# A gated mix of a state-space layer and linear attention: the skip term of seven late tiles moves from TensorE to VectorE, three more tiles are transposed by TensorE, and the late order is written anew

## The chip, the cores and the metric

The kernel runs on one core of one Trainium2 chip. The metric is the device time of one execution in microseconds (us), the median of several runs. The profile is of one execution, recorded by the hardware. A core has four engines that compute, each with its own queue worked off in order: TensorE (PE in the profile; PEld is its weight load), VectorE (DVE), ScalarE (ACT) and GpSimd (POOL). SyncE (SP) issues DMAs here; ScalarE and GpSimd issue some too.

## The reference

The input x has 2048 rows of 512. Two branches are computed from it and mixed by a gate for each row. In branch a, a diagonal complex recurrence of 512 states runs over the rows and is read out by C, and x times the vector Dskip is added. In branch b, 32 heads of linear attention use softmax features of both signs.

```python
g = _sigmoid((x * gate_w).sum(-1, keepdims=True))
# branch a
Lam_bar = jnp.exp(dt * Lam)
h = Lam_bar[None, :] * h + Bu[:, t, :]          # for each row t
y = 2.0 * jnp.einsum("blp,dp->bld", hseq, Cmat).real + x * Dskip[None, None, :]
# branch b
phi_q = jnp.concatenate([_softmax(pq, axis=-1), _softmax(-pq, axis=-1)], axis=-1)
kv = jnp.einsum("bhsf,bhsd->bhfd", phi_k, v)
o = num / den
return (lambda x, *d: x.transpose(*d))(o, 0, 2, 1, 3).reshape(B, S, D) @ wo
# the mix
return g * a + (1 - g) * b
```

## The kernel before

The rows are cut into 16 tiles of 128. A tile holds every eighth row: the rows of one residue r of 8, in one half a of the sequence. So the recurrence runs over one residue only and the others follow from it by matmuls. Output tile n is tile `order[n]` of the rows; the text below numbers tiles by n.

The program is written as generators (st_y, st_o and so on), each of which yields between steps. The long string ORDER (line 24) lists the steps, and the loop at line 817 walks it: a token such as "o7" runs the next step of that generator, "@7" names the PSUM bank that the step takes, ":D" puts an eviction on VectorE (otherwise it is ScalarE's), ":A" puts an output's DMA on ScalarE's queue (otherwise SP's). The order of ORDER is the order of each engine's queue. Waits between engines are put in from what each instruction reads and writes; a bank that is taken again is waited for until its last reader is done.

The first half of ORDER makes the weights, the keys' features, the values, the recurrence and the sums kv. The late part, from about 87 us on, makes the output:

- q n: four matmuls (128 rows by 512) into PSUM, evicted to row block n of Xq (bf16, 16 blocks of 512).
- X g, N g, E g, S g: the features of a group g of four tiles, from Xq's blocks 4g to 4g+3. X and N are trees of maxima and minima and a subtraction (VectorE, lines 512, 522 and 528), E is four exponentials (ScalarE, line 139), S is a tree of sums, its logarithm "lg", a difference "dl", its exponential "rho", a product (line 560) and four DMA transposes into phT, issued by SP (line 564). Group A is tiles 0 to 3.
- y n: branch a of tile n into one PSUM bank: eight matmuls over the states in two blocks of four (line 718), then four matmuls of 128 columns with the diagonal matrices Dd, which add x times Dskip (line 723).
- o n: the attention of tile n. For each half of the heads, four narrow matmuls into pn (line 737), then "ld" (a logarithm, always ScalarE) and "nu" (a copy out of PSUM, ScalarE or, with ":D", VectorE). Then "rd" (ScalarE), "on" (VectorE, line 745), and the transpose of on: a DMA transpose issued by SP (line 759), or for the tiles in OT_PE four TensorE transposes into a bank "po" (line 754) and a copy out of it.
- t n: four matmuls with Wo add the attention into y's bank (line 766); the sum times the gate G is evicted (line 778 on ScalarE, line 780 on VectorE) and stored (line 786). Tile LAST = 14 is evicted and stored in halves, one by ScalarE (line 772) and one by VectorE (line 773).
- G: the gate's value, four small steps; Y: the masked sums kv. h, c and z finish the recurrence.

The output leaves from PSUM bank to bank: y holds its bank from its first matmul to t's eviction. Eight banks serve q, h, y, pn and po.

Of the kernel before, what the change touches and what calls it, by code (L numbers as in the profile page):

```python
# [10 lines left out]
ALU = mybir.AluOpType  # L11
# [9 lines left out]
P = 128  # L21
# [18 lines left out]
h31@6 z3 z3 sA a4 h01 h31 c6 c6 sA q13@3 q13 z3 a4 a4 Y Y h22@0 G q10 z3 z3 G q6@2 q6 h22 z3 z3 sA sA Y Y c1 c1 q9@4  # L40
q8@6 q5@7 h62@3 h41@5 c3 h41 c1 c3 c3 h13@0 h62 q11@2 h13 q11 q8 q12@1 c6 q12 h21@5 q5 h21 h02@2 c7 q4@6 q4 h53@3 h53
h23@1 h23 h33@0 h33 sA q9 h40@7 h40 sA q7@5 h43@6 h63@3 c7 h43 q7 c7 y4@0 y4 sA h63 sA h03@1 END h02 o0@4 o0 X1 N1
o1@7 o1 q14@6 X1 N1 h03 o0@5 X1 o1@2 o1 o1 o0 o0 q15@3 o2@4 o2 o2@7 o2 N1 q15 X1 N1 X1 N1 E1 E1 y2@1 y1@2 y1 E1 E1 q14
# [26 lines left out]
def kernel(  # L70
# [641 lines left out]
    def st_y(n):  # L712
        ti = order[n]
        r, a = ti // 2, ti % 2
        py = bank([P, D], F32, "py")
        live["py", n] = py
        for t in range(NT2):
            MM(out=py[:], lhsT=hs(r, t, slice(a * P, (a + 1) * P)), rhs=C2B[t], start=(t == 0), stop=False)  # L718
            if t % 4 == 3:
                yield  # L720
        for kt in range(KT):
            xs = xT[:, kt, ti * P:(ti + 1) * P]
            MM(out=py[:, kt * P:(kt + 1) * P], lhsT=xs, rhs=Dd[:, kt, :], start=False, stop=False)  # L723
# [38 lines left out]
    def st_t(n):  # L762
        ti = order[n]
        py, oT = live["py", n], live["oT", n]
        for g in range(HG):
            MM(out=py[:], lhsT=oT[:, g, :], rhs=Wo[:, g, :], start=False, stop=(g == HG - 1))  # L766
        yield
        ot = pools["op"][1].tile([P, D], BF16, name="ot", bufs=14)
        ot2 = pools["op"][1].tile([P, D], BF16, name="ot", bufs=14) if n == LAST else ot

        def ot_halves():
            nc.scalar.mul(out=ot[:, 0:D // 2], in_=py[:, 0:D // 2], mul=G[:, ti:ti + 1])
            VS(out=ot2[:, D // 2:D], in0=py[:, D // 2:D], scalar1=G[:, ti:ti + 1], scalar2=None, op0=ALU.mult)

        if n == LAST:
            ot_halves()
        elif sel["eng"] == "act":
            nc.scalar.mul(out=ot[:], in_=py[:], mul=G[:, ti:ti + 1])  # L778
        else:
            VS(out=ot[:], in0=py[:], scalar1=G[:, ti:ti + 1], scalar2=None, op0=ALU.mult)  # L780
# [80 lines left out]
```

## Time and profile before

| what | us |
|---|---|
| median of 3 runs (155.09 to 156.0) | 155.27 |
| the profiled execution | 155.2 |
| its span | 153.1 |
| TensorE, busy in the span | 147.5 |
| VectorE | 133.1 |
| ScalarE | 129.3 |
| GpSimd | 15.8 |

Rows of the profile are read as follows. A row of the timeline gives the start, the duration, the engine, the line, the operation, what it writes and reads, and in brackets how long its engine had been idle before and what ended that. A row "x4" merges four instructions that follow one another. In a row of a group, "| 3.0, 748 |" is the total in us and the mean of one in ns, and behind it stands the idle time before such instructions. A row of the DMA issues ends with the size of one in KB and the us from issue to landing. In the chain of waits each row is a start, a length and what held the end up at that time; matmuls of one kind that follow one another stand as one row, at the pace at which they follow.

### The profile page before, as it was taken

The numbers are of one execution on the slowest core, as the hardware profiler recorded it, in microseconds if no ns is written. First come the engines' busy times: TensorE is split into PE (matmuls) and PEld (weight loads), VectorE is DVE, ScalarE is ACT, GpSimd is POOL, SyncE is SP. The second block draws the span as 40 slices with busy tenths as digits, with TensorE's granted clock in tenths as the row PEclk, the third lists the DMA queues.
The fourth block names the chain that finished last, engine by engine and source line by source line (L and its number), as shares of the span: only waits on it lengthen the run. The fifth ranks groups of instructions, "written<-read, shape, count | busy, mean of one in ns | idle before, by whom it ended". The sixth has DMA issues, their size and how long they took to land.

```text
span 153.1 us, 3382 instructions
## 1 busy us (share of the span) xinstructions
PE 147.5 (96%) x1254; PEld 95.5 (62%) x1254; DVE 133.1 (87%) x304; ACT 129.3 (84%) x279; POOL 15.8 (10%) x43
## 2 busy tenths in 40 slices
PE   7999979999999999999999999999999999999990
PEld 7844434788878986869867656555555555546550
DVE  3799999999999999999999999999999858716441
ACT  3589998999998999999998999699488998618471
POOL 8239980000000000000000000000000000000000
PEclk9999999999999999999999999999999999999999
DMA  4785996494455699720000007911159959989943
GB/s 122 158 215 77 232 160 143 99 79 104 103 107 100 133 222 178 167 97 4 0 0 4 0 0 167 76 37 33 36 98 144 178 125 187 168 139 186 255 145 104
DMA packets 50992, 17.55 MB, mean 115 GB/s; under 512 B 44192, under 2 KB 50976, under 8 KB 50976
## 3 DMA queue, kind: packets, MB, share of 16 engines
q1 hardware_dynamic: 49120, 15.82, 57.0%
q10 hardware_dynamic: 1696, 1.51, 3.1%
q8 instruction: 10, 0.16, 0.5%
q0 software_dynamic: 160, 0.01, 0.2%
q14 instruction: 6, 0.05, 0.2%
HBM read 2.64 MB, written 2.10 MB: 31 GB/s over the span
## 4 chain that ended last, share of the span: by engine, by line
PE 80%; SPq 9%; DMA 8%; issue 1%; DVE 0%; ACT 0%
PE pgq L602 18%; PE py L718 16%; PE py L766 9%; PE pq L476 9%; SPq L230 7%; DMA xT<-in_A_x_dram 5%; PE pk L476 5%; PE pv L476 5%; PE ph L669 4%; DMA phT<-EEq 3%; PE kvacc L579 3%; PE pn L737 3%; PE pgq L607 2%; PE py L723 2%; PE pgq L609 2%; SPq L285 1%
## 5 line engine op out<-in xcount | busy, mean ns | idle before, releaser
L602 PE MATMUL pgq<-xT,BT 128*128 128x256 bf16 x256 | 31.5, 273 | 0.0
L476 PEld LDWEIGHTS <-xT 128*128 128x128 bf16 x192 | 18.1, 97 | 19.2 <-DMA xT<-in_A_x_dram 1.7
L602 PEld LDWEIGHTS <-BT 128*128 128x128 bf16 x256 | 24.6, 98 | 4.1
L139 ACT ACTIVATE EEk<-EEk 128x1024 bf16<-128x1024 bf16 x20 | 20.5, 1082 | 0.0
L120 ACT CAST uv<-pgq 128x512 bf16<-128x512 f32 x28 | 15.9, 605 | 0.7 <-PE pgq L602 0.5
L766 PE MATMUL py<-Wo,oT 128*128 128x512 bf16 x64 | 15.9, 380 | 0.0
L476 PE MATMUL pv<-Wv,xT 128*128 128x512 bf16 x64 | 15.8, 379 | 0.0
L476 PE MATMUL pq<-Wq,xT 128*128 128x512 bf16 x64 | 15.6, 379 | 0.0
L476 PE MATMUL pk<-Wk,xT 128*128 128x512 bf16 x64 | 14.8, 380 | 0.8 <-DMA xT<-in_A_x_dram 0.8
L139 ACT ACTIVATE EEq<-EEq 128x1024 bf16<-128x1024 bf16 x12 | 11.7, 1043 | 0.2 <-DVE EEq L528 0.2
L139 ACT ACTIVATE ld<-pn 128x16 f32<-128x16 f32 x32 | 6.1, 191 | 6.1 <-PE pn L737 4.7
L778 ACT ACTIVATE ot<-py,G 128x512 bf16<-128x512 f32 x11 | 7.4, 689 | 4.0 <-PE py L766 3.6
L591 ACT ACTIVATE phT<-X,dgB 128x512 bf16<-128x512 bf16 x16 | 10.7, 725 | 0.0
L120 ACT CAST nu<-pn 128x256 bf16<-128x256 f32 x27 | 9.9, 381 | 0.0
L745 DVE TENSOR_TENSOR on<-nu,rd 128x512 bf16<-128x512 bf16 x16 | 6.7, 421 | 3.5 <-ACT rd L139 1.8
L120 ACT CAST Xq<-pk 128x512 bf16<-128x512 f32 x15 | 8.6, 597 | 1.3 <-PE pk L476 1.3
L120 ACT CAST vx<-pv 128x512 bf16<-128x512 f32 x16 | 9.1, 603 | 0.4 <-PE pv L476 0.4
L549 DVE TENSOR_TENSOR EEk<-EEk,rck 128x4096 bf16<-128x4096 bf16 (+1 forms) x5 | 9.3, 1859 | 0.0
L120 ACT CAST Xq<-pq 128x512 bf16<-128x512 f32 x16 | 8.9, 609 | 0.2 <-PE pq L476 0.2
L766 PEld LDWEIGHTS <-oT 128*128 128x128 bf16 x64 | 5.5, 97 | 5.7 <-DMA oT<-on 0.8
L737 PEld LDWEIGHTS <-phT 128*128 128x128 bf16 x128 | 6.3, 97 | 3.5 <-DMA phT<-EEq 0.8
L512 DVE TENSOR_TENSOR smk<-smk 128x512 bf16<-128x512 bf16 (+4 forms) x18 | 8.1, 447 | 0.1
(180 smaller groups left out, 323.9 us busy)
## 6 DMA issues: line engine op xcount, KB each, us to landing
X<-HM SPq DMA_DIRECT2D x8, 256.0 KB, 4.4
out_dram<-ot SPq DMA_DIRECT2D x8, 128.0 KB, 2.2
out_dram<-ot ACTq DMA_DIRECT2D x7, 128.0 KB, 2.7
C2r<-in_B_wqkv_dram ACTq DMA_DIRECT2D x2, 256.0 KB, 3.5
Wv<-in_B_wqkv_dram SPq DMA_DIRECT2D x1, 512.0 KB, 4.1
Bn<-in_A_B_re_dram SPq DMA_DIRECT2D x1, 512.0 KB, 6.4
Bn<-in_A_B_im_dram SPq DMA_DIRECT2D x1, 512.0 KB, 7.2
Wo<-in_B_wo_dram SPq DMA_DIRECT2D x1, 512.0 KB, 4.1
```

The source lines that it names most:

```text
L120: nc.scalar.copy(out=out_ap, in_=in_ap)
L139: ins = nc.scalar.activation(**kw)
L230: nc.sync.dma_start_transpose(out=xT[:, :, ti * P:(ti + 1) * P], in_=x_res[ti // 2, ti % 2])
L476: MM(out=pt[:], lhsT=xT[:, kt, ti * P:(ti + 1) * P], rhs=W[:, kt, :], start=(kt == 0), stop=(kt == KT - 1))
L512: VT(out=dst, in0=cur[:, :, :, 0:n, :], in1=cur[:, :, :, n:2 * n, :], op=op)
L549: VT(out=E5, in0=E5, in1=rc.to_broadcast([P, L, 2 * NB, Dh, 4]), op=ALU.mult)
L591: nc.scalar.mul(out=t_, in_=x_, mul=c_)
L602: MM(out=pg[:, h, :], lhsT=BT[:, kt, 2 * j + h, :], rhs=xT[:, kt, r * NC:(r + 1) * NC], start=(h == 0 and kt == 0), stop=(r % 2 == 0 and k ...
L718: MM(out=py[:], lhsT=hs(r, t, slice(a * P, (a + 1) * P)), rhs=C2B[t], start=(t == 0), stop=False)
L737: MM(out=pn[:, 4 * m:4 * m + 4, :].rearrange("p h e -> p (h e)"), lhsT=ph[:, 4 * hf + m, :], rhs=KVm[:, 4 * hf + m, :], start=(m == 0), st ...
L766: MM(out=py[:], lhsT=oT[:, g, :], rhs=Wo[:, g, :], start=False, stop=(g == HG - 1))
L778: nc.scalar.mul(out=ot[:], in_=py[:], mul=G[:, ti:ti + 1])
```

## The change

Seven of the late tiles, SKIP_DVE = (8, 9, 10, 11, 12, 13, 15), leave out the four Dskip matmuls of y. Their term x times Dskip times G is made by VectorE: step Z n computes it from x, G and Dskip into a float32 tile that lies in blocks 8 to 15 of Xq once these are read, and the eviction of t n becomes one VectorE instruction, py times G plus that tile. The x rows and Dskip, spread over the partitions, are loaded by three DMAs on GpSimd's queue (step XL, twice in the list) into blocks 0 to 7 of Xq.

The tuple OT_PE grows by tiles 8, 9 and 10, which are transposed by TensorE rather than by DMA. ORDER is the same up to its 499th token and new from there on. Among the new places: the first XL stands ahead of END and the second ahead of group 1's last steps; Z9 stands inside S3, the other Z between tiles 8's and 15's last steps; the list ends with t14, t13 and t15, where it ended with t15 and t14.

The late list is cut to its last part, before and after:

```diff
...
-y6@7 X3 t2:A o4@2 o4 o4@5 o4 o4 y6 y6 t3 X3 o4 X3 o4 S2 S2 t3 o5@1 o5 o5@2 o5 o5 y13@5 y13 o5 N3 o6@4 S2 o6 o6@1 o6 o6
-y12@2 o5 y7@4 y7 y12 o6 o6 t4 y7 S2 S2 t4:D S2 E3 E3 E3 E3 S2 o7@1 o7 t5 t5 S3 o7@0 o7 S3 o7 t6 S3 o7 S2 o7 y8@1 o8@3
...
-o11 y15 o13@4 o13:D o13@6 t6:A o13 o13 o11 o12 y10@1 o14@4 y15 o14:D o12@6 t9 o12:D t7:A t1 y10 y10 o13 o15@4 o15
-o15@6 t4:A t5 o15 o15 t8 o15 t12 t12 t12:A t10 o14@4 o14 o14 t10:D o13@6 t11 o15@2 o15 t10 o13:D t11 t11:A y13 t13 o14
-o14@1 t15 t13 t13 t15 t15 o14:D t14 t14 t14:A
...
+h23 c7 sA q8@1 h43@0 h62@5 q12@4 h41 h43 h62 sA q7 c7 sA h03@6 q8 h21@1 h63 h03 XL h21 END y5@5 o1@2 X1 o0@6 o0 N1 o1
+y6@0 o0@6 o2@1 X1 y6 o1@2 o2 N1 X1 N1 X1 o0 q14@7 N1 o2@6 o0 o1 X1 o1 y1@2 y0@1 y1 N1 q12 XL X2 h02 q14 y4@7 o1 y2@3
...
+o4@3 o4 X3 S2 y5 y7 N3 S2 y3 o3 o5@3 o4 o4 S2 o5 N3 S1 o5@1 o5 S2 y7 S1 y14@3 t3 o6@1 S2 o5 S2 o5 E3 o6 y6 y14 o6@1 S2
+o4 t3:D y14 o5 o7@4 t4 E3 o6 y13@1 o6 t5 E3 E3 o7:D S2 t4:D y11@7 o8@4 t5 S2 o6 o8 o7@5 y11 o7 S3 o8@4 o9@5 o9 o8 o7
+Z9 S3 y13 S3 S3 o9@5 o9:D S3 o8 S3 o6 o7 S2 S3 t6 S2 S3 t6 y10@5 o10@4 o8 o10 y10 o10@4 o10:D o7 y9@0 o10 Z8 S3 o9 Z11
+o8@4 o8 y9 o11@4 o9 t8 o11 o9@4 o10 t7 t8:D S3 o9 o10@4 t9 S3 o10:D o12@4 Z12 t7 Z10 o12 o11@2 y15@6 S3 o12@4 o11:D
+o11 t10 o13@2 o11 y15 t9:D o11 t2:A t10:D t6:A o12 o14@4 o13:D o12 o14:D t0:A o14@0 o14 t9 o12 y12@5 o14 o13@4 o15@2
+o12@0 o15 o14 o12:D t1 y12 t10 t7:A t3 o13 Z13 t5 o15@2 o15:D o13 t11 o14@4 o15 o14 o13 t12 t8 o15 o15@4 t11:D t12:D
+o13@2 o15:D t4:A t14 o13 t11:A Z15 t12:A t14 t13 t15 t14:A t13:D t15:D t13 t15
-OT_PE = (12, 13, 14, 15)
+OT_PE = (8, 9, 10, 12, 13, 14, 15)
 LAST = 14
+SKIP_DVE = (8, 9, 10, 11, 12, 13, 15)
+GX_SLOT = (0, 1, 2, 3, 0, 1, 0)
...
             MM(out=py[:], lhsT=hs(r, t, slice(a * P, (a + 1) * P)), rhs=C2B[t], start=(t == 0), stop=False)
             if t % 4 == 3:
                 yield
+        if n in SKIP_DVE:
+            return
         for kt in range(KT):
             xs = xT[:, kt, ti * P:(ti + 1) * P]
             MM(out=py[:, kt * P:(kt + 1) * P], lhsT=xs, rhs=Dd[:, kt, :], start=False, stop=False)
+        yield
+
+    def st_XL():
+        rows = x2.rearrange("(a c r) d -> c a r d", r=NR, c=P)
+        nc.gpsimd.dma_start(out=Xq[:, 0:3, :], in_=rows[:, 0, 0:5:2])
+        nc.gpsimd.dma_start(out=Xq[:, 3, :], in_=A_Dskip.unsqueeze(0).to_broadcast([P, D]))
+        yield
+        nc.gpsimd.dma_start(out=Xq[:, 4:8, :], in_=rows[:, 1, 0:7:2])
+        yield
+
+    def st_Z(n):
+        ti = order[n]
+        k = GX_SLOT[SKIP_DVE.index(n)]
+        gx = Xq[:, 8 + 2 * k:10 + 2 * k, :].rearrange("p a d -> p (a d)").bitcast(F32)
+        live["gx", n] = gx
+        nc.vector.scalar_tensor_tensor(out=gx, in0=Xq[:, 4 * (ti % 2) + ti // 4, :], scalar=G[:, ti:ti + 1], in1=Xq[:, 3, :], op0=ALU.mult, op1=ALU.mult)
         yield
 
...
         if n == LAST:
             ot_halves()
+        elif n in SKIP_DVE:
+            nc.vector.scalar_tensor_tensor(out=ot[:], in0=py[:], scalar=G[:, ti:ti + 1], in1=live["gx", n], op0=ALU.mult, op1=ALU.add)
         elif sel["eng"] == "act":
             nc.scalar.mul(out=ot[:], in_=py[:], mul=G[:, ti:ti + 1])
         else:
...
```

More of the change, by code (lines that the diff above doesn't have):

```diff
@@ L39 @@
 eA g73 g73 q10@5 sA h11@0 h11 O h00@4 g73 sA v13@2 h00 v13 a4 z3 sA v15@6 z3 v15 h20@0 h01@4 h30@2 v14 h20 sA h30 z3
[L40 to L43, printed above, removed]
@@ L44 @@
-X2 y0@5 y0 o1 y4 X2 N2 X2 o0 o0 o3@4 o3 o3@7 o3 o1 o3 y2 X2 N2 o2 X2 N2 S1 S1 N2 S1 o3 S1 N2 S1 S1 o3 y5@3 o2 o2 S1 S1
-S1 y1 E2 E2 E2 E2 y9@6 G N3 y5 y5 y3@4 y2 X3 X3 N3 t1 G t1 N3 S1 N3 S2 y9 y9 S2 S2 S1 S1 S2 y3 y3 t3 y0 t0 t0 t2 t2
-y6@7 X3 t2:A o4@2 o4 o4@5 o4 o4 y6 y6 t3 X3 o4 X3 o4 S2 S2 t3 o5@1 o5 o5@2 o5 o5 y13@5 y13 o5 N3 o6@4 S2 o6 o6@1 o6 o6
-y12@2 o5 y7@4 y7 y12 o6 o6 t4 y7 S2 S2 t4:D S2 E3 E3 E3 E3 S2 o7@1 o7 t5 t5 S3 o7@0 o7 S3 o7 t6 S3 o7 S2 o7 y8@1 o8@3
-t6 o8 o8@0 o8 o8 S3 S3 y12 t0:A y11@7 o8 o8 o9@3 o9:D o9@0 o9:D S3 y8 y8 o9 o9 S3 S3 o9 o10@3 y11 o10 o10@0 y11 o10
@@ L49 @@
-o10 S3 y14@3 S3 y14 t7 t7:D t8 y14 t8 y15@0 o11@4 S3 o11 o11@1 t9 o12@4 o11:D o11 S3 o10 o10 o12 o12@1 o12 o12 t9:D
-o11 y15 o13@4 o13:D o13@6 t6:A o13 o13 o11 o12 y10@1 o14@4 y15 o14:D o12@6 t9 o12:D t7:A t1 y10 y10 o13 o15@4 o15
-o15@6 t4:A t5 o15 o15 t8 o15 t12 t12 t12:A t10 o14@4 o14 o14 t10:D o13@6 t11 o15@2 o15 t10 o13:D t11 t11:A y13 t13 o14
-o14@1 t15 t13 t13 t15 t15 o14:D t14 t14 t14:A
+h31@6 z3 z3 sA a4 h01 h31 c6 c6 sA q13@3 q13 z3 a4 a4 Y Y h22@0 G q10 z3 z3 G q6@2 q6 q9@7 Y z3 h02@3 c3 q11@5 z3 Y c6
@@ new lines @@
+h22 sA q11 q4@2 sA c3 h53@5 h53 h13@0 c1 h40@1 c3 sA q4 c1 q9 q7@6 h33@4 c7 h33 q5@5 h41@7 h13 h40 h23@0 c1 h63@2 q5
+h23 c7 sA q8@1 h43@0 h62@5 q12@4 h41 h43 h62 sA q7 c7 sA h03@6 q8 h21@1 h63 h03 XL h21 END y5@5 o1@2 X1 o0@6 o0 N1 o1
+y6@0 o0@6 o2@1 X1 y6 o1@2 o2 N1 X1 N1 X1 o0 q14@7 N1 o2@6 o0 o1 X1 o1 y1@2 y0@1 y1 N1 q12 XL X2 h02 q14 y4@7 o1 y2@3
+X2 N2 o3@4 o2 E1 X2 o1 o0 X2 E1 y1 y0 y0 E1 o0 N2 X2 E1 o3 S1 o2 S1 y2 S1 N2 S1 t1 N2 q15@4 o2 S1 G o3@6 y4 q15 t0 y5
+o3 S1 o2 y2 S1 N2 S1 S1 G y3@4 y8@6 N3 o3 X3 N3 t2 E2 E2 X3 o3 E2 E2 y3 t1 t2 t0 y8 X3 N3 S1 y7@2 y4 o4@1 X3 o4 S2
@@ L791 @@
     st = {"V": st_V(), "V2": st_V2(), "U": st_U(), "P": st_P(), "P2": st_P2(), "P3": st_P3(), "P4": st_P4(), "B": st_B(), "gw": st_gw(),
-          "M": st_M(), "D": st_D(), "L": st_L(), "G": st_G(), "Y": st_Y(), "END": st_END(), "NR": st_N(0), "NI": st_N(1), "O": st_O()}
+          "M": st_M(), "D": st_D(), "L": st_L(), "G": st_G(), "Y": st_Y(), "END": st_END(), "NR": st_N(0), "NI": st_N(1), "O": st_O(), "XL": st_XL()}
     for n in range(8, NTI):
@@ L805 @@
     for n in range(NTI):
-        st.update({f"k{n}": st_k(n), f"v{n}": st_v(n), f"q{n}": st_q(n), f"y{n}": st_y(n), f"o{n}": st_o(n), f"t{n}": st_t(n)})
+        st.update({f"Z{n}": st_Z(n), f"k{n}": st_k(n), f"v{n}": st_v(n), f"q{n}": st_q(n), f"y{n}": st_y(n), f"o{n}": st_o(n), f"t{n}": st_t(n)})
     for n, (t0_, L_) in enumerate(KG):
```

## The prediction

> **What bounds it now.** I read the page first, then the busy time in stretches of the second half, then the chain of waits.
>
> ```profile
> span 153.1 us, 3382 instructions
> PE 147.5 (96%) x1254; PEld 95.5 (62%) x1254; DVE 133.1 (87%) x304; ACT 129.3 (84%) x279; POOL 15.8 (10%) x43
> PE 80%; SPq 9%; DMA 8%; issue 1%; DVE 0%; ACT 0%
> ```
> ```profile
> core 0: us, PE busy (x) PEld busy (x) DVE busy (x) ACT busy (x) POOL busy (x), PEclk, DMA share, GB/s
> 110.00:115.00 5.00, 5.00 (x36) 2.69 (x34) 4.93 (x10) 3.90 (x6) 0.00 (x0) 1.00 0.62 80
> 125.00:130.00 5.00, 5.00 (x44) 2.76 (x43) 3.67 (x6) 4.61 (x14) 0.00 (x0) 1.00 0.89 166
> 130.00:135.00 5.00, 5.00 (x44) 2.81 (x43) 2.94 (x6) 2.65 (x12) 0.00 (x0) 1.00 1.01 145
> 135.00:140.00 5.00, 4.99 (x40) 2.47 (x38) 2.21 (x5) 2.54 (x10) 0.00 (x0) 1.00 0.94 175
> 140.00:145.00 5.00, 5.00 (x55) 3.00 (x54) 2.22 (x6) 2.44 (x12) 0.00 (x0) 1.00 0.94 224
> 145.00:150.00 5.00, 4.52 (x35) 2.27 (x31) 2.27 (x5) 4.12 (x10) 0.00 (x0) 1.00 0.47 158
> ```
>
> TensorE holds 80% of the chain and is busy in all but a sliver of every stretch up to 149.5 us, at a granted clock of 1.00. VectorE is as full at 110 to 115 us (4.93 of 5), but from 125 to 150 it is busy 13.3 of 25 us. So the time is TensorE's work plus its waits plus a tail. The chain gives the price of each step of that work and the tail:
>
> ```profile
> 125.98 0.22 PE py L723 x4
> 128.19 0.86 PE py L718 x4
> 129.05 0.25 PE pn L737 x8
> 138.06 0.86 PE py L766 x4
> 145.07 0.22 PE po L754 x4
> 149.53 0.02 issue
> 149.56 0.48 ACT ot L772
> 150.06 0.48 DVE ot L773
> ```
>
> **The change, part by part.** All times are against this execution: span 153.1 us, 155.2 us in all, so 2.1 us lie around the span; the median of the runs is 155.27, the same within their spread.
>
> *TensorE's work.* Seven tiles lose their four Dskip matmuls: 7 x 0.22 = 1.54 us less. Three tiles (8, 9, 10) get four transposes each: 3 x 0.22 = 0.66 us more. Net 0.88 us less, all of it on the path, since TensorE waits for next to nothing. Even with no new wait, then, 0.88 us is most of what there is to win.
>
> *A new wait at y11.* I followed the late list queue by queue. Its tight place is "E3 E3 o7:D S2 t4:D y11@7". Tile 11's y takes bank 7 again, which holds tile 4's sum until t4's eviction, and that is now on VectorE behind o7's eviction, also on VectorE. These rows say what o7's waits for:
>
> ```profile
> 119.24 0.42 DVE L745 TENSOR_TENSOR on<-nu,rd 128x512 bf16<-128x512 bf16 x1 [0.25 <-ACT rd L139]
> 120.72 0.28 DVE L554 TENSOR_TENSOR dlq<-lgq 128x128 f32<-128x128 f32 x1
> 121.11 0.42 DVE L745 TENSOR_TENSOR on<-nu,rd 128x512 bf16<-128x512 bf16 x1
> 121.45 1.22 DVE L528 TENSOR_TENSOR EEq<-mnq,Xq 128x2048 bf16<-128x2048 bf16 x1
> 138.54 0.42 DVE L122 CAST nu<-pn 128x256 bf16<-128x256 f32 x1 [2.08 <-ACT ld L139]
> 138.88 0.41 DVE L745 TENSOR_TENSOR on<-nu,rd 128x512 bf16<-128x512 bf16 x1
> ```
> ```profile
> 121.03 0.31 ACT L139 ACTIVATE rhoq<-dlq 128x128 bf16<-128x128 f32 x1
> 121.58 0.18 ACT L139 ACTIVATE ld<-pn 128x16 f32<-128x16 f32 x1 [0.23 <-PE pn L737]
> 121.91 0.20 ACT L139 ACTIVATE ld<-pn 128x16 f32<-128x16 f32 x1
> 122.23 0.43 ACT L139 ACTIVATE rd<-ld,nge 128x128 bf16<-128x128 f32 x1
> 122.70 3.90 ACT L139 ACTIVATE EEq<-EEq 128x1024 bf16<-128x1024 bf16 x4
> 126.50 0.16 ACT L139 ACTIVATE ld<-pn 128x16 f32<-128x16 f32 x1
> 138.30 0.20 ACT L139 ACTIVATE ld<-pn 128x16 f32<-128x16 f32 x1
> ```
>
> The cast of nu on VectorE starts when ScalarE's ld from the same bank has ended (138.50, then 138.54). In the new list o7's ld stands on ScalarE behind all four exponentials of E3, which wait for N3's last step (L528). That ran at 121.45. The new list has VectorE's same instructions ahead of it, less S2's dl (0.39 to the next row) and one "on" (0.34): about 120.6, or 120.2 if the 0.25 wait and other short ones go too. I take 120.4. Then N3's step and dl behind it take 1.22 and 0.28 (121.85), and rho 0.21 on ScalarE (its 0.31 less the overlap that neighbours show), so E3 starts at about 122.05. Four exponentials take 3.80 (122.70 to 126.50) and o6's steps between them 0.33 + 0.32 + 0.31 = 0.96: o7's ld starts at 126.8 and ends at 127.0. The cast takes 0.34 (138.54 to 138.88) and t4's eviction 0.75 (L780 below): bank 7 is free at about 128.1, bounds 127.6 and 128.4.
>
> When does TensorE want it? From y11 on the new list holds 21 blocks of four wide matmuls (11 of y, 10 of t), 17 half tiles of o and 7 sets of transposes: 21 x 0.86 + 17 x 0.13 + 7 x 0.22 = 21.8 us. Without new waits it would end at 149.53 - 0.88 = 148.65, so it reaches y11 at 148.65 - 21.8 = 126.85. It waits 128.1 - 126.85 = 1.25 us, bounds 0.75 and 1.55. Waits that I see ahead of it (y14 for bank 3 behind o5's eviction, some 0.4) shorten this one and cost nothing more. Queued behind y11 is everything left on TensorE; no slack follows.
>
> *Short turnarounds after it.* y10 for bank 5, the transposes of 8 and of 12, and t13 each come just as their bank or input is freed, about 0.1 each: 0.4 us, bounds 0 and 0.8.
>
> *The tail.* The last tile is now 15, evicted whole by VectorE and stored by one DMA of 128 KB, where before tile 14 went in halves, ScalarE's and then VectorE's.
>
> ```profile
> out_dram<-ot SPq DMA_DIRECT2D x8, 128.0 KB, 2.2
> out_dram<-ot SPq DMA_DIRECT2D x1, 64.0 KB, 1.6
> oT<-on SPq DMA_TRANSPOSE x12, 2.7
> phT<-EEq SPq DMA_TRANSPOSE x12, 3.3
> vec_m<-in_A_Dskip_dram POOLq DMA_DIRECT2D x1, 1.0 KB, 3.1
> ```
> ```profile
> L780 DVE TENSOR_SCALAR ot<-py,G 128x512 bf16<-128x512 f32 x4 | 3.0, 748 | 4.1 <-PE py L766 4.1
> L778 ACT ACTIVATE ot<-py,G 128x512 bf16<-128x512 f32 x11 | 7.4, 689 | 4.0 <-PE py L766 3.6
> L449 DVE SCALAR_TENSOR_TENSOR psi<-iot,ssm_par,kk 128x256 f32<-128x256 f32 x4 | 1.9, 474 | 0.0
> ```
>
> Before, TensorE's end to VectorE's end took 149.53 to 150.54, 1.0 us; now 0.75 and some 0.05. The landing goes from 1.6 to 2.2. Sum: -0.25 + 0.6 = +0.35, bounds 0 (the landings alike) and 0.9 (the store of tile 13, just ahead on SP's queue, in its way).
>
> *VectorE's and ScalarE's work.* Each new product x*Dskip*G has two tensors in and float32 out: nearest is L449, 474 ns for half as wide, so 0.80 us if the other 256 elements cost what L780's 512 (748) cost over the cast's 256 (0.42), 0.33 (bounds 0.42, as a bf16 product of 512 like "on", and 0.95, twice 474). Seven make 5.6 us. The seven skip tiles' evictions all lie on VectorE: nine whole evictions there now against four, 5 x 0.75 = 3.7 us; two nu more, 0.8. I cost it at nothing beyond the above, since 11.7 us of the 25 from 125 on were idle; 13.3 + 5.6 + 3.7 + 0.8 = 23.4 leaves 1.6 us idle, and that cover is thin (a rival). ScalarE loses five evictions of 0.69 and gains three copies of transposed tiles; no wait ends on it late.
>
> *Queues.* SP issues three row transposes fewer; but t6's rows now wait for "on" of tile 6, behind t4's eviction, and the last two transposes of group 2 stand behind them in SP's queue. With 3.3 us to land, tile 10's arrive close to when o10 wants them: in the range, not in the sum.
>
> *The x loads.* The last of group 1's reads in Xq:
>
> ```profile
> 101.70 1.22 DVE L528 TENSOR_TENSOR EEq<-mnq,Xq 128x2048 bf16<-128x2048 bf16 x1
> ```
>
> Three DMAs of about 1 MB on GpSimd's queue, which issues nothing else by then. The first waits for reads of Xq's rows 0 to 3, past before the late list; the second for group 1's reads, which end at 102.9 here. The row of a small POOLq load has 3.1 us to landing, a large store 2.2, so it lands by 110; Z9, its first reader, comes at about 129. The Trainium skill (SBUF — State Buffer, Summary: rules for kernel authors) speaks against this: descriptors of a GpSimd DMA are starved while VectorE runs in its wider perf modes, so such a load should be issued from ScalarE or SP. By that rule the sum stays the same so long as the load lands before Z9; no run here shows it.
>
> **Sum:** -0.88 + 1.25 + 0.4 + 0.35 = +1.1 us: 155.2 + 1.1 = 156.3 us.
>
> **The rivals.**
>
> *The wait doesn't bite* (o7's cast not held by ld, or ScalarE through E3 by 125.5). Then -0.88 + 0.35 + 0.2 = 154.9; 154.3 with the tail alike. Against it are the rows at 138.30 and 138.54; for it, that TensorE waited for almost nothing in the old list, whose y also took banks closely. Not slower; chance 0.20.
>
> *VectorE becomes the bound from 127 us on.* The 23.4 us of 25 above are in order, and where its evictions free banks each delay reaches TensorE. It decides once the products and the evictions with the added term cost 0.95 in place of 0.80 and 0.75: 7 x 0.15 + 7 x 0.20 = 2.45 us, of which the idle time hides 1.2 (the rest of it being waits for ScalarE and TensorE), so +1.25 over the sum: 157.6, up to 159. For it: its idle time falls from 11.7 us to 1.6; against it: products and evictions are placed in its gaps, ahead of their use. Chance 0.24.
>
> *The loads are late.* If VectorE's dense stretch kept GpSimd from issuing until VectorE first idles (about 124), a load landing at 131 or later holds Z9, and behind it S3, whose rows have some 2 us of slack. Landing at 133.7, it costs 2.7 - 1.0 = 1.7 us over the sum: 158. For it: VectorE's 4.93 of 5 us; against it: 3.1 us to landing for a small load, with 26 us of room. Chance 0.06. The Trainium skill's rule above would lead here only at its worst.
>
> The forecast keeps 0.50, with its own range 155.4 to 157.1.
>
> **How the numbers follow.** One per cent, about what a measurement of this kernel tells from no change, is 153.7 to 156.8. Faster than that needs 1.5 us, more than the 0.88 removed: 0.05, out of the first rival. Slower: a quarter of the forecast's half (0.13), the second rival but its lightest cases (0.20) and the third: 0.39. The rest, 0.56, is no change. The range 154.4 to 158.2 leaves out the best of the first rival and the worst of the others, under 2 in 10.
>
> **What would show it.** Right: the group of Dskip matmuls at 36 in place of 64; TensorE idle for about a microsecond near 127 ahead of y11, released by VectorE's eviction of py; VectorE's cast of nu just ahead of it released by ScalarE's ld; the last eviction on VectorE at 512 wide, with its store landing in over 2 us. Wrong: TensorE full to the end; or waits spread over 130 to 148 with VectorE at 9 tenths or more (the second rival); or VectorE's product waiting for a DMA into Xq (the third).

## The result, and the profile after

Seven runs of the changed kernel have a median of 156.62 us (156.23 to 157.01), seven of the kernel before beside them 155.06 (154.54 to 156.0): the ratio is 1.0088, interval 1.0062 to 1.0114. The change costs about 1.4 us. The profiled execution took 156.62 us, its span 154.9, where that of before took 155.2 and 153.1.

The page of the changed kernel, the lines that answer to those of before (the chain of waits last). Line numbers have moved by 2 up to y's matmuls over the states and by 4 to 22 behind them:

```profile
span 154.9 us, 3351 instructions
PE 145.2 (94%) x1220; PEld 94.4 (61%) x1238; DVE 141.2 (91%) x318; ACT 127.9 (83%) x275; POOL 17.9 (12%) x46
PE 63%; SPq 10%; DVE 10%; DMA 7%; ACT 4%; issue 3%; ACTq 0%; DVEq 0%
```

TensorE has less work than before and a smaller share of the chain (80% then); VectorE and ScalarE now hold 14% of it together, where each had 0%. The stretches from 125 us on say where:

```profile
core 0: us, PE busy (x) PEld busy (x) DVE busy (x) ACT busy (x) POOL busy (x), PEclk, DMA share, GB/s
125.00:130.00 5.00, 3.79 (x24) 1.81 (x24) 2.66 (x5) 3.33 (x9) 0.00 (x0) 1.00 0.57 106
130.00:135.00 5.00, 5.00 (x41) 2.58 (x40) 4.57 (x9) 3.82 (x16) 0.00 (x0) 1.00 0.82 155
135.00:140.00 5.00, 4.95 (x43) 2.79 (x42) 4.07 (x8) 3.00 (x8) 0.00 (x0) 1.00 1.12 142
140.00:145.00 5.00, 4.95 (x52) 2.85 (x50) 4.66 (x11) 3.35 (x16) 0.00 (x0) 1.00 0.87 215
145.00:150.00 5.00, 4.95 (x36) 2.59 (x35) 4.77 (x11) 2.68 (x8) 0.00 (x0) 1.00 0.67 226
```

TensorE loses 1.2 us in the first stretch and next to nothing after it, though VectorE is then busy for 4.07 to 4.77 us of each 5. In the first stretch VectorE itself is busy for only 2.66 of 5 us: it waits too. Three timelines show for what. TensorE's three late waits that the rows name, and the row ahead of the last (the bracket holds the idle time before the row and what ended it):

```profile
108.48 1.04 PE L786 MATMUL py<-Wo,oT 128*128 128x512 bf16 x4 [0.35 <-DMA oT<-on]
120.96 1.02 PE L720 MATMUL py<-C2r,Bn 128*128 128x512 bf16 x3 [0.18 <-ACT nu L122]
...
126.29 1.03 PE L786 MATMUL py<-Wo,oT 128*128 128x512 bf16 x4
128.47 1.02 PE L720 MATMUL py<-C2r,Wv 128*128 128x512 bf16 x4 [1.16 <-DVE ot L802]
```

VectorE:

```profile
120.70 1.22 DVE L530 TENSOR_TENSOR EEq<-mnq,Xq 128x2048 bf16<-128x2048 bf16 x1
...
127.34 0.42 DVE L124 CAST nu<-pn 128x256 bf16<-128x256 f32 x1 [2.95 <-ACT ld L141]
127.68 0.74 DVE L802 TENSOR_SCALAR ot<-py,G 128x512 bf16<-128x512 f32 x1
...
129.80 0.75 DVE L743 SCALAR_TENSOR_TENSOR Xq<-Xq,G 128x512 f32<-128x512 bf16 x1
```

ScalarE:

```profile
122.37 1.04 ACT L141 ACTIVATE EEq<-EEq 128x1024 bf16<-128x1024 bf16 x1
...
125.21 2.02 ACT L141 ACTIVATE EEq<-EEq 128x1024 bf16<-128x1024 bf16 x2
127.11 0.20 ACT L141 ACTIVATE ld<-pn 128x16 f32<-128x16 f32 x1
```

Read from the bottom up: the last two exponentials of E3 end where ld starts, ld's end starts VectorE's copy of nu after 2.95 us of idling, behind the copy stands t4's eviction of py, and its end at 128.42 starts the matmuls of y11. The first product, Z9, comes at 129.80.

The bracket counts from the end that the profile gives the matmul before, and so it leaves out 0.16 us of each such wait. Four matmuls of 512 columns follow one another in 0.86 us. So y11 could have started at 126.29 + 0.86 = 127.15 and started at 128.47: counted from starts, the wait is 1.32 us, where the bracket has 1.16. Below, "by starts" means this way of counting: how much further apart two neighbouring matmuls start than matmuls of their kind do (0.216 us at 512 columns, 0.056 at 128). Gaps of exactly one matmul are left out, since some matmul records are missing from the trace.

To set the executions side by side I count from a point that comes before any difference in TensorE's list, the start of the last group of gate matmuls (kvacc from gw_b): 86.43 us before, 86.63 after. The 0.20 between them is no part of the change; over all the kernels run here it goes from 85.9 to 86.9.

| us | before | after | difference |
|---|---|---|---|
| that point to TensorE's end | 63.09 | 63.97 | +0.87 |
| TensorE's end to the span's end | 3.62 | 4.27 | +0.64 |

The span grew from 153.14 to 154.86 us, by 1.72: 0.20, 0.87 and 0.64 with rounding (the differences are taken before the times are rounded). The medians differ by 1.56.

### The profile page after: what moved, and what is told of

Its sections match the earlier page's. It is cut to its first block, busy times and chain, and to the rows that moved or that the text cites. A ratio compares the mean times of both kernels' runs of the same rounds, so it can differ in the third digit from the quotient of the medians.

```text
span 154.9 us, 3351 instructions
## 1 busy us (share of the span) xinstructions
PE 145.2 (94%) x1220; PEld 94.4 (61%) x1238; DVE 141.2 (91%) x318; ACT 127.9 (83%) x275; POOL 17.9 (12%) x46
## 4 chain that ended last, share of the span: by engine, by line
PE 63%; SPq 10%; DVE 10%; DMA 7%; ACT 4%; issue 3%; ACTq 0%; DVEq 0%
PE pgq L604 18%; PE py L720 10%; SPq L232 8%; PE pq L478 7%; PE py L786 5%; PE pv L478 4%; DMA xT<-in_A_x_dram 4%; PE pk L478 4%; PE ph L671 3%; PE kvacc L581 3%; DMA oT<-on 3%; ACT EEq L141 2%; PE pgq L609 2%; DVE ot L798 2%; PE pgq L611 2%
## 5 line engine op out<-in xcount | busy, mean ns | idle before, releaser
L757 PEld LDWEIGHTS <-phT 128*128 128x128 bf16 x128 | 7.0, 98 | 4.9 <-DMA phT<-EEq 0.2
L122 ACT CAST nu<-pn 128x256 bf16<-128x256 f32 x25 | 9.1, 375 | 0.0
L757 PE MATMUL pn<-KVm,phT 128*128 128x68 bf16 x128 | 7.8, 194 | 0.0
```

Of the source, the lines that this page charges most:

```text
L122: nc.scalar.copy(out=out_ap, in_=in_ap)
L757: MM(out=pn[:, 4 * m:4 * m + 4, :].rearrange("p h e -> p (h e)"), lhsT=ph[:, 4 * hf + m, :], rhs=KVm[:, 4 * hf + m, :], start=(m == 0), st ...
```

## The experiments

Ratios are to the kernel before, timed on the same chip in five rounds; its medians were 154.78, 155.41, 155.04 and 155.01 us in the four groups. "TensorE's part" and "the tail" are the two rows of the table above.

### First group: the wait, VectorE, the tail, the loads

**o7's copy by ScalarE.** The copy of nu that stood on VectorE ahead of t4's eviction goes to ScalarE.

```diff
-o4 t3:D y14 o5 o7@4 t4 E3 o6 y13@1 o6 t5 E3 E3 o7:D S2 t4:D y11@7 o8@4 t5 S2 o6 o8 o7@5 y11 o7 S3 o8@4 o9@5 o9 o8 o7
+o4 t3:D y14 o5 o7@4 t4 E3 o6 y13@1 o6 t5 E3 E3 o7 S2 t4:D y11@7 o8@4 t5 S2 o6 o8 o7@5 y11 o7 S3 o8@4 o9@5 o9 o8 o7
```

> The changed kernel with one token changed: o7's first copy of nu is ScalarE's again (o7 in place of o7:D), so t4's eviction no longer stands behind it on VectorE. Theory (the wait at y11 holds the end up): t4's sum was ready at about 125.5 us, so its eviction ends near 126.4 and y11 starts when TensorE comes to it, at 127.2 in place of 128.47. TensorE's 1.16 us wait goes, nothing else close behind takes its place, and the end moves by 0.9 to 1.3 us: about 155.4 us, ratio to before 1.002. Rival (VectorE's fuller list from 130 us on is the bound): the start is earlier but VectorE, at 4.6 of 5 us, loses it again; 156.2 or more.

154.77 us, ratio 1.0004 (0.9984 to 1.0025). The timelines of this kernel, VectorE's and then TensorE's:

```profile
124.61 0.75 DVE L802 TENSOR_SCALAR ot<-py,G 128x512 bf16<-128x512 f32 x1 [1.24 <-PE py L786]
...
126.14 1.03 PE L720 MATMUL py<-C2r,Wv 128*128 128x512 bf16 x4
```

t4's eviction now starts as soon as TensorE has its sum, and y11 starts at 126.14 without a wait. TensorE's part is 62.51 us, 1.46 less than the 63.97 of the changed kernel. So the chain through VectorE's queue cost 1.3 us (1.0088 less 1.0004, of 155) to 1.46, and without it the kernel is level with the one before: its TensorE's part is 0.58 us shorter than before the change (63.09), and its tail, 4.26 us, is 0.64 longer.

**No product.** The seven products are left out and the seven tiles evicted plainly, so x times Dskip is missing from those tiles.

```diff
-        nc.vector.scalar_tensor_tensor(out=gx, in0=Xq[:, 4 * (ti % 2) + ti // 4, :], scalar=G[:, ti:ti + 1], in1=Xq[:, 3, :], op0=ALU.mult, op1=ALU.mult)
...
-            nc.vector.scalar_tensor_tensor(out=ot[:], in0=py[:], scalar=G[:, ti:ti + 1], in1=live["gx", n], op0=ALU.mult, op1=ALU.add)
+            VS(out=ot[:], in0=py[:], scalar1=G[:, ti:ti + 1], scalar2=None, op0=ALU.mult)
```

> The changed kernel without the seven products x*Dskip*G and with plain evictions of py times G in their place: it leaves the Dskip term of seven tiles out. VectorE has 7 x 0.66 = 4.6 us less to do from 129 us on; the list, the loads and the wait at y11 are as they were. Theory (wait at y11, then TensorE's work, then the tail): the wait stays at about 1.2 us and the end moves by less than 0.4 us: 156.2 to 156.7. Rival (VectorE is the bound late): 1 us or more faster, 155.6 or less.

156.03 us, ratio 1.0075 (1.0048 to 1.0103). The wait at y11 stays:

```profile
127.72 1.02 PE L720 MATMUL py<-C2r,Wv 128*128 128x512 bf16 x4 [1.15 <-DVE ot L801]
```

VectorE's line of the page falls from 141.2 to 136.5 us, and the time by some 0.2, less than the intervals: VectorE's load is not what the change pays for.

**Tile 15 in halves.** The last tile is evicted by two instructions of VectorE and stored by two DMAs of 64 KB, on ScalarE's and SP's queues.

```diff
...
+        elif n == 15:
+            for o_, s_ in ((ot, slice(0, D // 2)), (ot2, slice(D // 2, D))):
+                nc.vector.scalar_tensor_tensor(out=o_[:, s_], in0=py[:, s_], scalar=G[:, ti:ti + 1], in1=live["gx", n][:, s_], op0=ALU.mult, op1=ALU.add)
...
-        if n == LAST:
+        if n in (LAST, 15):
...
```

> The changed kernel with the last tile (15) evicted by VectorE in two halves of 256, each stored by its own DMA of 64 KB (ScalarE's queue and SP's). Theory: of the span's growth 0.7 us is the tail (TensorE's end to the span's end 3.6 us before, 4.3 now), because a 128 KB store ends later than a 64 KB one. The second half ends 0.1 us later than the whole did, the store lands 0.7 to 0.9 sooner: 155.9 to 156.1 us. Rival (the tail is set by SP's second issue or by whatever lies behind the last store): no change, 156.5 or more.

156.00 us, ratio 1.0073 (1.0043 to 1.0103). The time lies in the range expected, but the kernel before, too, was 0.28 us faster in this group than beside the first runs (154.78 against 155.06); by the ratios the gain is 0.2 us. The tail went from 4.27 to 4.02 us, not by the 0.5 to 0.7 expected. A miss; its cause comes out below.

**The loads alone.** The kernel before, with the three loads issued at about the same places of its list (two XL tokens) and read by nothing.

```diff
+        nc.gpsimd.dma_start(out=Xq[:, 0:3, :], in_=rows[:, 0, 0:5:2])
+        nc.gpsimd.dma_start(out=Xq[:, 3, :], in_=A_Dskip.unsqueeze(0).to_broadcast([P, D]))
...
+        nc.gpsimd.dma_start(out=Xq[:, 4:8, :], in_=rows[:, 1, 0:7:2])
```

> The kernel before with the three x and Dskip loads on GpSimd's queue added and read by nobody. Theory: GpSimd and the DMA queues are idle enough where they run (issued at 76 and 104 us in the changed kernel, landing in 3.5 to 4.1 us), so nothing moves: 155.1, ratio 0.998 to 1.003. Rival (the loads disturb VectorE's dense stretch or the row transposes): slower by 0.5 us or more.

154.91 us, ratio 1.0009 (0.9983 to 1.0035): no cost that the timing can tell. Its tail, though, is 3.99 us against 3.62, which I understood only with the last run.

### Second group: another cure, and each half of the change undone

**o7 first.** The same wait taken away in another way: o7's step and t4's eviction stand ahead of the last two exponentials, and VectorE keeps the copy.

```diff
-o4 t3:D y14 o5 o7@4 t4 E3 o6 y13@1 o6 t5 E3 E3 o7:D S2 t4:D y11@7 o8@4 t5 S2 o6 o8 o7@5 y11 o7 S3 o8@4 o9@5 o9 o8 o7
+o4 t3:D y14 o5 o7@4 t4 E3 o6 y13@1 o6 t5 o7:D t4:D E3 E3 S2 y11@7 o8@4 t5 S2 o6 o8 o7@5 y11 o7 S3 o8@4 o9@5 o9 o8 o7
```

> The changed kernel with two steps moved, none changed in kind: o7's first half and t4's eviction stand ahead of the last two exponentials of E3 in the list, so that o7's copy stays on VectorE but its ld on ScalarE no longer waits for two exponentials (1.9 us). Theory (VectorE's copy was held by ld, ld by the exponentials): ld runs at about 125.2 us in the changed kernel's time in place of 127.1, t4's eviction ends 1.9 us sooner, y11 doesn't wait, and the end moves as much as in the run that gave the copy to ScalarE, 1.1 to 1.4 us: ratio 0.998 to 1.002. Rival (it was VectorE's own work in front of the eviction, the copy's 0.34 us): at most 0.4 us of it goes, ratio 1.006 or more.

155.02 us, ratio 0.9984 (0.9957 to 1.001). Its timelines, ScalarE, VectorE and TensorE:

```profile
124.84 0.20 ACT L141 ACTIVATE ld<-pn 128x16 f32<-128x16 f32 x1
...
125.08 0.42 DVE L124 CAST nu<-pn 128x256 bf16<-128x256 f32 x1 [1.06 <-ACT ld L141]
125.42 0.74 DVE L802 TENSOR_SCALAR ot<-py,G 128x512 bf16<-128x512 f32 x1
...
126.78 1.03 PE L720 MATMUL py<-C2r,Wv 128*128 128x512 bf16 x4
```

The copy is still on VectorE and still released by ld, but ld comes 2.3 us sooner, and TensorE doesn't wait at y11. So the copy's own 0.34 us on VectorE was not the cost. It took both links: the copy ahead of t4's eviction on VectorE, and the exponentials ahead of ld on ScalarE. The run with the copy on ScalarE took away the first and this one the second, and either was enough.

**Dskip back on TensorE.** The kernel with o7's copy on ScalarE, with the 28 Dskip matmuls of the seven tiles again and no products; the loads are still issued.

```diff
...
-            if t % 4 == 3:
+            if t == 3 or t == 7 and n not in SKIP_DVE:
                 yield
-        if n in SKIP_DVE:
-            return
...
```

> The run with o7's copy on ScalarE, with the seven tiles' Dskip matmuls on TensorE again (at the end of each y) and without the products on VectorE; the loads are still issued, the list is the same. Theory (TensorE's work plus its waits sets the end): 7 x 0.22 = 1.54 us come back on TensorE, 1.3 to 1.6 us of it at the end: 156.2, ratio 1.008 to 1.012. Rival (VectorE's relief of 4.6 us pays part of it back): under 1 us, ratio 1.006 or less.

156.81 us, ratio 1.0081 (1.0053 to 1.0108). TensorE's part is 64.08 us against 62.51 with the same list: 1.57 for 28 matmuls, 0.056 each. So on TensorE the part of the change that was to gain does gain, in full; by the ratios of the two kernels (1.0081 and 1.0004, on two chips) the time rose by 1.2 us.

**Tiles 8 to 10 by DMA.** The same kernel with these tiles' rows transposed by DMA again, as before the change; their steps for the TensorE transposes leave the list.

```diff
...
-OT_PE = (8, 9, 10, 12, 13, 14, 15)
+OT_PE = (12, 13, 14, 15)
...
```

> The run with o7's copy on ScalarE, with tiles 8, 9 and 10 transposed by DMA again (SP, at the same places of the list), so 0.66 us less on TensorE. Theory: in this list SP's queue is taken by group 3's four transposes from about 132.4 to 138 us in that run's time, tile 8's rows land some 2 us after t8 wants them, and the later ones push group 3's: TensorE waits 2 to 3.5 us, ratio 1.008 to 1.018. Rival (SP has room, since three of its twelve transposes less were enough before): 0.66 us faster, ratio 0.996.

158.61 us, ratio 1.0201 (1.0173 to 1.0228), more than expected. The two waits of TensorE that are new, from its timeline:

```profile
138.26 2.54 PE L794 MATMUL py<-Wo,oT 128*128 128x512 bf16 x11 [2.82 <-DMA oT<-on]
145.52 0.43 PE L765 MATMUL pn<-KVm,phT 128*128 128x68 bf16 x8 [1.43 <-DMA phT<-EEq]
```

The list places t8 to t10 for rows that TensorE transposes. By DMA they come 2.8 us late, and the features' transposes stand behind them on SP's queue. TensorE is spared 0.66 us of transposes and waits 4.25 by the brackets, 4.57 by starts; its part is 66.52 us against 62.51.

**Both.** o7 first and tile 15 in halves, their diffs together.

> The moved steps (o7's first half and t4's eviction ahead of the last two exponentials) together with the last tile's eviction and store in halves. Theory (the two add, since one is a wait ahead of y11 and the other lies behind TensorE's end): the gain of the moved steps, 1.1 to 1.4 us, and the 0.24 us by which the halves shortened the time behind TensorE's end: ratio 0.997 to 0.999, 154.5 us, at or just under the kernel before. Rival (they overlap): 1.000 or more.

155.19 us, ratio 0.999 (0.9962 to 1.0018), no better than o7 first alone (0.9984). The tail is 4.01 us against 4.27 there and TensorE's part 62.56 against 62.43, so the trace shows a gain in the tail that the times do not tell from none.

### Third and fourth group: the tail

**Tile 13's store on ScalarE's queue.** The kernel with both, and one token more.

```diff
-o13@2 o15:D t4:A t14 o13 t11:A Z15 t12:A t14 t13 t15 t14:A t13:D t15:D t13 t15
+o13@2 o15:D t4:A t14 o13 t11:A Z15 t12:A t14 t13 t15 t14:A t13:D t15:D t13:A t15
```

> The kernel of the run with o7 first and tile 15 in halves, with one edit more: tile 13's store is issued on ScalarE's queue rather than SP's, so that SP's queue holds nothing just ahead of tile 15's second half. Theory that the tail's halves gained only 0.24 us because tile 13's 128 KB store stood just ahead on the same queue: the time from TensorE's end to the span's end falls from 4.05 to about 3.6 us, as before the change (3.62), and the ratio to the kernel before is about 0.995 to 0.997. Rival, that the store of tile 13 costs by the bytes in flight whatever its queue, or that two steps on VectorE and the landing are what is left: tail 3.9 to 4.2 us, ratio 0.998 to 1.000.

155.14 us, ratio 1.0002 (0.9974 to 1.0031), tail 4.01 us: the same. My theory of the store just ahead on SP's queue falls.

**Tile 14 last.** o7 first, and the end in the order t15, t13, t14.

```diff
-o12@0 o15 o14 o12:D t1 y12 t10 t7:A t3 o13 Z13 t5 o15@2 o15:D o13 t11 o14@4 o15 o14 o13 t12 t8 o15 o15@4 t11:D t12:D
-o13@2 o15:D t4:A t14 o13 t11:A Z15 t12:A t14 t13 t15 t14:A t13:D t15:D t13 t15
+o12@0 o15 o14 o12:D t1 y12 t10 t7:A t3 o13 Z13 t5 o15@2 o15:D o13 t11 o14@4 o15 o14 o13 t12 t8 o15 o15@4 o15:D t11:D t12:D
+o13@2 t4:A t15 o13 t11:A Z15 t12:A t15:D t13 t14 t15 t13:D t14 t13:A t14:A
```

> The kernel with o7 ahead of the last two exponentials, its end put in another order: t15's matmuls ahead of t13's and t14's, so that tile 14 ends the program in two halves (ScalarE's, then VectorE's) as it does in the kernel before, and tile 13's store goes on ScalarE's queue. Theory, that the tail's 0.64 us come from ending with a whole tile on VectorE and one 128 KB store: TensorE's end to the span's end is about 3.6 us (3.62 before, 4.26 after), and unless the transposes of tile 15, now wanted at once, hold TensorE (0 to 0.4 us), the ratio to the kernel before is 0.994 to 0.998. Rival, that the tail is set by the store of tile 13 or 15 just ahead: tail over 3.9 us, ratio 0.998 to 1.001.

156.39 us, ratio 1.0068 (1.0035 to 1.0101). TensorE waited 0.52 us for tile 15's rows, tile 14's half stood behind tile 13's eviction on VectorE and its store behind tile 13's on ScalarE's queue, and the tail was 4.81 us. A bad edit; it says little of the theory.

**o7 first, again.**

> The kernel with o7 and t4's eviction ahead of the last two exponentials, once more, beside the two kernels with another end on the same chip: ratio to the kernel before 0.996 to 1.001, tail 4.2 to 4.3 us; the other two are to be read against it. If the theory of the tail holds, both lie 0.002 to 0.004 below it; by its rival all three are alike within 0.0015.

155.31 us, ratio 0.9998 (0.9966 to 1.0029), tail 4.27 us. The two runs of this kernel, 0.9984 and 0.9998, differ by less than their intervals.

So I took the tail apart. Behind the last store the program closes: SyncE waits in turn for the semaphores that tell of a DMA's landing, the engines pass an instruction that the trace calls DRAIN, and GpSimd clears the semaphores and lets the others go. The views leave these instructions out, but the trace holds their times:

```
us                                    before  loads  after  15 in halves  o7 first and halves
TensorE's end to the last landing       2.70   2.70   2.80          2.62                 2.62
last landing to SyncE's first drain     0.08   0.08   0.26          0.21                 0.21
first drain to the span's end           0.84   1.20   1.20          1.19                 1.19
sum                                     3.62   3.99   4.27          4.02                 4.01
a step of GpSimd in the last part      0.078  0.453  0.453         0.444                0.444
```

The store itself ends 0.10 us later than before, and the other 0.54 are in the closing. Of these, 0.36 come in every kernel that has the three loads on GpSimd, the old list with unread loads among them. That called for the last run.

**The loads by SyncE.** The kernel with both; the three loads keep their places in the list and go to SyncE's queue.

```diff
-        nc.gpsimd.dma_start(out=Xq[:, 0:3, :], in_=rows[:, 0, 0:5:2])
-        nc.gpsimd.dma_start(out=Xq[:, 3, :], in_=A_Dskip.unsqueeze(0).to_broadcast([P, D]))
+        nc.sync.dma_start(out=Xq[:, 0:3, :], in_=rows[:, 0, 0:5:2])
+        nc.sync.dma_start(out=Xq[:, 3, :], in_=A_Dskip.unsqueeze(0).to_broadcast([P, D]))
...
-        nc.gpsimd.dma_start(out=Xq[:, 4:8, :], in_=rows[:, 1, 0:7:2])
+        nc.sync.dma_start(out=Xq[:, 4:8, :], in_=rows[:, 1, 0:7:2])
```

> The kernel with o7 first and tile 15 in halves, its three x and Dskip loads issued by SyncE at the same places of the list rather than by GpSimd. In every kernel so far that has the three loads, the one in which nothing reads them among them, the closing steps of the program, from SyncE's first drain to the span's end, take 1.19 to 1.20 us against 0.84 in the kernel before, and the 0.36 us more lie between two semaphore steps of GpSimd (442 to 453 ns against 78). Theory, that those 0.36 us belong to GpSimd's longer instruction list and not to the stores: the closing steps take 0.84 us again, the time from TensorE's end to the span's end falls from 4.02 to about 3.65, and the ratio to the kernel before is 0.995 to 0.998, if the loads cost SyncE's queue nothing (it issues nothing between about 98 and 104 us, where the first two fall; the third, at about 104, has 0.4 us of a transpose's issue behind it). Rival, that the 0.36 us come with the loads whoever issues them, or with something else in the new list: closing steps 1.2 us, ratio 0.998 to 1.001. Second rival, that the transposes on SyncE's queue come late: a wait of TensorE for oT between 104 and 112 us, ratio above 1.000.

154.87 us, ratio 0.9988 (0.9966 to 1.0011). SyncE's timeline shows the loads' issues between its transposes:

```profile
92.26 6.45 SPq L566 DMA_TRANSPOSE phT<-EEk  x4
98.76 0.58 SPq L732 DMA_DIRECT2D Xq<-in_A_x_dram  x1
99.39 1.89 SPq L733 DMA_DIRECT2D Xq<-in_A_Dskip_dram  x1
103.53 0.62 SPq L735 DMA_DIRECT2D Xq<-in_A_x_dram  x1
104.43 7.64 SPq L779 DMA_TRANSPOSE oT<-on  x3
```

The closing from the first drain is 0.84 us again and GpSimd's step 0.078: the theory of that step holds, and the wait for late transposes (the second rival) isn't there. But the ratio is not in the range expected, as the tail is 3.96 us and not 3.65: from the last landing to the first drain it now takes 0.53 us. SyncE's waits show why. It goes through the DMAs' semaphores in a fixed order that ends with 109, and takes 59 to 69 ns for each step behind the last store's. In these traces the DMAs that SyncE and ScalarE issue late in the program take the semaphores 100, 102 and 104 to 109 in turn, so one such DMA more or less moves the last store on or back by a place: three transposes less put it at 106, one store more at 107, three loads on SyncE beyond that at 100. GpSimd's DMAs have others, so three loads there leave it at 109:

```
kernel                  the last store's semaphore   waits behind it   landing to first drain, us
before                                         109                 0                         0.08
loads alone (GpSimd)                           109                 0                         0.08
tiles 8 to 10 by DMA                           109                 0                         0.08
both (o7, halves)                              107                 2                         0.21
after                                          106                 3                         0.26
loads by SyncE                                 100                 7                         0.53
```

A version of the last kernel whose last store has number 109 would by these rows end 0.45 us sooner; it wasn't run. None of the versions that ran beats the kernel before by more than the intervals.

## Why the prediction was right

The forecast was +1.1 us by four terms; the mechanism that decides, the new wait at y11, was right in place, chain and nearly in size. One term, the tail, was mis-sized, and for a reason that the prediction didn't have. Another, the short turnarounds, was too large and made good by a second error, which is luck.

**TensorE's work, -0.88: right.** These groups of the changed kernel have the counts foreseen (PE's Dskip matmuls and transposes, then VectorE's new evictions and products; total in us and mean in ns behind the bar):

```profile
L727 PE MATMUL py<-Dd,xT 128*128 128x128 bf16 x36 | 3.5, 219 | 0.0
L774 PE MATMUL po<-ident,on 128*128 128x128 bf16 x28 | 2.5, 219 | 0.0
...
L798 DVE SCALAR_TENSOR_TENSOR ot<-py,G,Xq 128x512 bf16<-128x512 f32 x7 | 5.1, 746 | 0.0
L743 DVE SCALAR_TENSOR_TENSOR Xq<-Xq,G 128x512 f32<-128x512 bf16 x7 | 5.0, 745 | 0.0
```

Putting the 28 matmuls back cost 1.57 us for the 1.54 worked out.

**The wait at y11, +1.25 with bounds 0.75 and 1.55: right.** Step by step:

| step, us | predicted | measured |
|---|---|---|
| N3's last step starts | 120.4 | 120.70 |
| E3 starts | 122.05 | 122.37 |
| o7's ld ends | 127.0 | 127.31 |
| bank 7 is free | 128.1 | 128.42 |
| TensorE reaches y11 | 126.85 | 127.15 by starts (127.31 by the bracket) |
| wait | 1.25 | 1.32 by starts (1.16 by the bracket) |

All the times lie 0.30 to 0.32 late, of which 0.20 is the execution's own start. (A slip in the working, 120.4 + 1.22 + 0.28 = 121.85 where it is 121.90, is inside the bounds.) Both cures gave it back. TensorE's part fell by 1.54 us to 62.43 with o7 first: 1.32 for this wait, and 0.22 because the wait for a DMA transpose near 108 us, which differs between executions, was 0.29 by starts there and 0.51 in the changed kernel. With the copy on ScalarE it fell by 1.46: 1.32, and 0.28 near 108 us, less 0.15 of short losses that the changed kernel doesn't have, with rounding.

**Short turnarounds, +0.4: too large, made good by luck.** I had put them behind y11, at y10, the transposes of 8 and 12 and t13. By starts TensorE lost 0.09 us at y10 and 0.03 at the transposes of 8, and not as much as 0.03 at any other place behind y11: 0.12 in all. The 21.8 us for the matmuls from y11 on were 0.2 too few instead. So from bank 7's release to TensorE's end the sum is right, 21.8 + 0.4 = 22.2 against 150.60 - 128.42 = 22.18, with two errors that cancel.

Ahead of y11, TensorE lost 0.51 us by starts at 108.48 for a DMA transpose of on, which was not foreseen; 0.35 at 120.96, where y14 takes bank 3 behind o5's copy of nu, as foreseen at some 0.4; and 0.19 at 124.44. The kernel before lost 0.66 us by starts over the same part of its list. Such a wait shortens the one at y11, as the prediction says, since bank 7's release sets y11's start. Once the wait at y11 is gone they count: TensorE's part is then 0.58 to 0.67 us below the kernel before and not the 0.88 of the work, and the longer tail takes that away.

**The tail, +0.35 with bounds 0 and 0.9: mis-sized, +0.64.** The two parts that I summed were -0.25 and +0.6. TensorE's end to the last issue went from 1.06 to 0.82 us, as said. From issue to landing the last store went from 1.64 to 1.98 (the prediction took 2.2, the median of all, and wanted over 2 as a sign), so 0.34 for the 0.6. Together they are 0.10. The other 0.54 are the closing of the program: 0.18 for the place of the last store's semaphore, 0.36 for GpSimd's step. The prediction took the span's end for the store's landing and a constant, and it isn't constant. The 0.29 that this term is short is about what the forecast is short of the measured 1.4.

**VectorE's products and evictions at nothing: right.** A product took 745 ns (0.80 taken) and an eviction with the added term 746, as much as the plain one. VectorE was busy 20.7 of the 25 us from 125 on, where I had 23.4, and without the products the time fell by some 0.2 us, which the intervals don't tell from none. The second rival is refuted: its point was 0.95 a piece, and it wanted TensorE's waits spread over 130 to 148 us, where by starts they come to 0.12, though VectorE was at 9 tenths or more in three of the four stretches from 130 us on.

**The loads: right.** The DMA issues of the changed kernel (size in KB and us to landing at the end):

```profile
Xq<-in_A_x_dram POOLq DMA_DIRECT2D x1, 512.0 KB, 4.1
Xq<-in_A_x_dram POOLq DMA_DIRECT2D x1, 384.0 KB, 3.5
...
out_dram<-ot SPq DMA_DIRECT2D x8, 128.0 KB, 2.4
out_dram<-ot SPq DMA_DIRECT2D x1, 64.0 KB, 1.7
```

The larger was issued at 103.8 us, in a stretch in which VectorE was busy for 4.96 of 5 us:

```profile
104.00:109.00 5.00, 4.60 (x31) 2.28 (x31) 4.96 (x10) 3.80 (x7) 0.58 (x1) 1.00 0.63 157
```

It landed by 108, and Z9 read it at 129.8. Issued by SyncE it took 3.9 us for the same 512 KB. The rule of the Trainium skill (SBUF — State Buffer, Summary: rules for kernel authors), that a GpSimd DMA starves under VectorE's wide modes, is not borne out by this load: 4.1 against 3.9 us with VectorE at 4.96 of 5. But all ten of VectorE's instructions there are TENSOR_TENSOR in bf16, and the trace doesn't name the mode of an instruction, so other instructions may do what these did not. (The third rival's price takes 1.0 us off where it names some 2 us of slack; nothing came of it.)

**The first rival, that the wait doesn't bite,** had 154.9 us. The kernels that lack the wait and have nothing of the change undone took 154.77 to 155.31, the one with tile 14 last aside.

## What to carry to other kernels

When work moves from a full engine to one with room, the price is not the room but the order: follow the moved instruction's neighbours on its new queue back to what each waits for. Here a copy of 0.42 us, held by an instruction that stood behind four exponentials, cost 1.3 us, where the 28 matmuls less the transposes had gained 0.9. And what is won ahead of the last matmul can be lost behind it (here 0.64 us), so account for the end of the program apart, from the last matmul to the last landing and from there to the end.

## What was not expected of the hardware

- The closing of the program took 0.92 us from the last landing to the span's end before the change and 1.47 after. One step of GpSimd in it took 0.44 to 0.45 us in all the kernels with the three loads on its queue and 0.078 in the two without, so it goes with what GpSimd has to do (64 recorded instructions there, 69 with the loads: three DMA issues and two semaphore instructions more). Which of these makes it longer stays open: number and kind were not told apart, nor the three further semaphores that the loads use there.
- SyncE's closing waits run through the DMA semaphores in a fixed order, and by the last store's place in it the time from its landing to SyncE's first drain was 0.08 to 0.53 us.
- The 384 KB load took 3.5 us to land when GpSimd issued it at 76 us and 5.1 when SyncE did at 98.8, both just ahead of the load of Dskip; the place in the program differs too, so the queue isn't shown as the cause. The 512 KB one, at 104 us in both cases, took 4.1 and 3.9.
